# Issue order of the load queue, earlier Strassen inputs and a later output product in a two-MoE kernel

## The chip, the cores and the metric

The kernel runs on one core of one Trainium2 chip. The metric is device time in microseconds (us) of one execution. A core has five engines with a queue of instructions each: TensorE (PE, matrix products), VectorE (DVE), ScalarE (ACT), GpSimd (POOL) and SyncE (SP), which here issues nearly all DMA transfers. Each engine works through its own queue in order; engines wait for each other on semaphores.

## The reference

```python
def reference(q, k, v, w_in, w_out, w_gate, w_val, w_out2, rms_g):
    # 4 batches, 8 heads, 576 positions, head size 64
    # heads 0-3: the last 32 positions; heads 4-7: every 32nd position
    attn = softmax_masked(q @ k.T / 8) @ v
    x = attn as 2304 tokens x 512
    h = x @ w_in                              # 512 x 2048
    x = (h - np.tanh(h)) @ w_out              # 2048 x 512   (MoE one)
    xn = x / sqrt(mean(x * x) + 1e-6) * rms_g # MoE two
    g, val = xn @ w_gate, xn @ w_val          # 512 x 1536 each
    return (g * sigmoid(g) * val) @ w_out2    # 1536 x 512
```

All is fp32. The weights arrive as float64.

## The kernel before

Every fp32 operand is split into a high and a low part, and a product is made of three matmuls. A weight tile (128 x 512 numbers of 64 bits, 512 KB) is loaded as `raw`, turned into fp32 by ACT (a Prelu, L171 or L277) and DVE (L177, L178 or L278, L279), and split by ACT, DVE and POOL.

The program has four stages. Attention fills the gaps of **MoE one**, which runs in five groups of tokens; the last group (`g == NG - 1`, f = 0 to 15) lasts from about 374 to 462 us of the span. It prepares MoE two: `prep` loads the first 512 tokens' `x2d`, forms their sums of squares, 1/sqrt by three Newton steps on 128 x 512 elements, and `xn`. Its last results leave by ACT copies `xe` and transfers `x2d<-xe`.

**The plain stage** (462 to 573.5 us) runs MoE two on these 512 tokens in `FB` = 12 tiles f. `pe_gv(0, f)` makes the gate (`ps_h`) and the value (`ps_m`) of a tile and `p`, the product of silu(gate) and value; `pe_o(0, f)` adds the tile's 12 output matmuls into four banks `ps_x` (L927 and L928 split `p`). `Store` writes each decoded weight to DRAM (L343), `Decode.to` loads and decodes the weights of the next stage, and `both_preps` makes that stage's inputs: `prep_s` for the norm of 896 tokens, `conv(m)` for the inputs `xt[m]`.

**Two Strassen passes** (j = 0, 1) of 896 tokens follow, each of six pairs of tiles. A pair has seven products m, in the order 1, 2, 5, 6, 3, 7, 4, of 12 matmuls 128 x 448 (`both`: 6 for the gate, 6 for the value), and seven outputs `out(t)` of six matmuls 128 x 512, which are made during the next pair. Two tiles of a pair are turned by `Pair.steps` into the sums `wo`; nine blocks w_0 to w_8 of each pair go to DRAM (`Store`, or `put` at L255) and come back as `wt` (`fetch`, L260). `keep` copies a product out of its banks: `u<-ps_pr` on ACT (L1102). `second` stands in the first pair of the first pass, after product 1: it makes the last output matmuls of the plain stage, `pe_o(0, FB - 1)`, and `evac_o` copies the four banks `ps_x` to two buffers `o`, tiles 0 and 2 on ACT (L946), 1 and 3 on DVE (L948), each followed by its transfer `out_dram<-o` (L949). Product 6 writes into the banks that `keep` has to read after product 1:

```python
self.both(1, P, True)
if (self.j, self.p) == (0, 0):
    second()
m1 = self.keep(P)
...
self.both(6, P, False)
```

The order on each engine is that of the scheduler, which sorts instructions by its own estimate of time, except under `tc.manual_schedule(engines=...)`, where the named engines keep the order of the program. Before the change PE alone is held to it, in the first groups of MoE one and in the Strassen passes. `wts` is a pool of 22 rooms of 4 KB a partition (`tag="w"`), shared by weights and by the temporaries `wa`, `ws`, `s2` and `tr`.

Of the kernel before, what the change touches and what calls it, by code (L numbers as in the profile page):

```python
# [33 lines left out]
def attn_moe_moe_kernel(  # L34
# [211 lines left out]
    class Pair:  # L246
# [21 lines left out]
        def steps(self):  # L268
            a, t = {}, {}

            def bits(kd, i):
                if i == 0:
                    a[kd] = wts.tile([128, 2, 512], F32, tag="w", name="wa")
                w = self.ws[2 * kd + i].raw.rearrange("p c f -> p (c f)").bitcast(U32).rearrange("p (n t) -> p n t", t=2)
                lo, hi = w[:, :, 0], w[:, :, 1].bitcast(F32)
                o = a[kd][:, 1 - i].bitcast(U32)
                nc.scalar.activation(out=hi, in_=hi, func=ACTF.Prelu, scale=2.0 ** -111, alpha=-(2.0 ** 32))  # L277
                nc.vector.tensor_scalar(out=o, in0=lo, scalar1=29, scalar2=None, op0=ALU.logical_shift_right)  # L278
                nc.vector.scalar_tensor_tensor(  # L279
                    out=o, in0=hi.bitcast(U32), scalar=3, in1=o, op0=ALU.logical_shift_left, op1=ALU.bitwise_or  # L280
                )

            def sums(kd):
                t[kd] = wts.tile([128, 4, 256], F32, tag="w", name="ws")
                x = [a[kd][:, k // 2, 256 * (k % 2):256 * (k % 2) + 256] for k in range(4)]
                y = [t[kd][:, k] for k in range(4)]
                for o, p, q, op in (
                    (0, x[0], x[1], ALU.add), (1, y[0], x[2], ALU.subtract),
                    (2, x[2], x[0], ALU.subtract), (3, x[3], y[1], ALU.subtract),
                ):  # L290
                    nc.gpsimd.tensor_tensor(out=y[o], in0=p, in1=q, op=op)

            def half(kd, n):
                self.part(2 + 2 * n + kd, t[kd][:, 2 * n:2 * n + 2].rearrange("p n f -> p (n f)"))

            for kd in range(2):
                yield 2 * kd, lambda: bits(kd, 0)
# [563 lines left out]
    def prep():
        n = R0
        x2 = pbx.tile([128, 4, 2 * HT], F32, tag="x2", name="x2")[:, :, :n]
        for c in range(4):
            nc.sync.dma_start(out=x2[:, c, :], in_=x2d[c * 128:c * 128 + 128, 0:n])
        acc = pbx.tile([128, 512], F32, tag="acc", name="acc")[:, :n]
        sq = pbx.tile([128, 512], F32, tag="sq", name="sq")[:, :n]
        yield
        nc.scalar.activation(out=acc, in_=x2[:, 0], func=ACTF.Square)
        for c in range(1, 4):  # L870
            nc.scalar.activation(out=sq, in_=x2[:, c], func=ACTF.Square)
            nc.vector.tensor_tensor(out=acc, in0=acc, in1=sq, op=ALU.add)
            yield
        s2 = wts.tile([128, 2, 512], F32R, tag="w", name="s2")
        nc.scalar.copy(out=s2[:, 0], in_=acc)
        nc.vector.tensor_tensor(out=s2[:, 1], in0=acc, in1=s2[:, 0].bitcast(F32), op=ALU.subtract)
        yield
        ps = ps_m.tile([128, 512], F32, tag=nth("m", 2), name="ps_m")[:, :n]
        mm(ps, ones, s2[:, 0], True, False)
        mm(ps, ones, s2[:, 1], False, True)  # L880
        yield
        m, y = acc, sq
        z = pbx.tile([128, 512], F32, tag="z", name="z")[:, :n]
        nc.vector.tensor_scalar(
            out=m, in0=ps, scalar1=1.0 / DM, scalar2=1.0e-6, op0=ALU.mult, op1=ALU.add
        )
        yb, zb = y.bitcast(I32), z.bitcast(I32)
        nc.vector.tensor_scalar(
            out=zb, in0=m.bitcast(I32), scalar1=1, scalar2=None, op0=ALU.logical_shift_right
        )  # L890
        nc.vector.tensor_scalar(
            out=yb, in0=zb, scalar1=-1.0, scalar2=float(0x5F3759DF), op0=ALU.mult, op1=ALU.add
        )
        for _ in range(3):
            yield
            nc.vector.scalar_tensor_tensor(out=z, in0=y, scalar=-0.5, in1=y, op0=ALU.mult, op1=ALU.mult)
            nc.vector.tensor_tensor(out=z, in0=z, in1=m, op=ALU.mult)
            nc.vector.scalar_tensor_tensor(out=y, in0=z, scalar=1.5, in1=y, op0=ALU.add, op1=ALU.mult)
        yield
        t = mid.tile([128, 2, 4, 512], F32R, tag="xs", name="xn")  # L900
        for c in range(4):
            nc.vector.scalar_tensor_tensor(
                out=x2[:, c, :], in0=x2[:, c, :], scalar=gcol[:, c:c + 1], in1=y,
                op0=ALU.mult, op1=ALU.mult,
            )
            nc.scalar.copy(out=t[:, 0, c], in_=x2[:, c])
            nc.vector.tensor_tensor(out=t[:, 1, c], in0=x2[:, c], in1=t[:, 0, c].bitcast(F32), op=ALU.subtract)
            yield
        xn[0] = t

    p_of, oacc = {}, {}

    def pe_gv(j, f):
# [9 lines left out]
                s = pb.tile([128, 512], F32, tag="s", name="s")[:, :n]  # L923
                nc.scalar.activation(out=s, in_=ps, func=ACTF.Silu, scale=WS)
        nc.vector.scalar_tensor_tensor(out=s, in0=r[1], scalar=WS, in1=s, op0=ALU.mult, op1=ALU.mult)
        t = pb.tile([128, 2, 512], F32R, tag="p", name="p")[:, :, :n]
        nc.scalar.copy(out=t[:, 0], in_=s)  # L927
        nc.vector.tensor_tensor(out=t[:, 1], in0=s, in1=t[:, 0].bitcast(F32), op=ALU.subtract)  # L928
        p_of[j, f] = t
# [18 lines left out]
                nc.vector.tensor_scalar_mul(out=o, in0=oacc[j][t], scalar1=WS)  # L948
            nc.sync.dma_start(out=out[t * 128:t * 128 + 128, :], in_=o)  # L949

    xt = {}

    def prep_s(j, bank):
        base = R0 + 2 * HT * j
        x = pbx.tile([128, 4, 2 * HT], F32, tag="x2", name="x2")
        for c in range(4):
            nc.sync.dma_start(out=x[:, c], in_=x2d[c * 128:c * 128 + 128, base:base + 2 * HT])
        xt["raw"] = x
        yield
        parts = [(0, 512), (512, 2 * HT)]  # L960
        m, y, z = (pbx.tile([128, 8], F32, tag=n, name=n) for n in ("rm", "ry", "rz"))
        nt = 2 * HT // 128
        m, y, z = m[:, :nt], y[:, :nt], z[:, :nt]
        for h, (a, e) in enumerate(parts):
            n = e - a
# [2 lines left out]
            for c in range(1, 4):  # L968
                nc.scalar.activation(out=sq, in_=x[:, c, a:e], func=ACTF.Square)
                nc.vector.tensor_tensor(out=acc, in0=acc, in1=sq, op=ALU.add)  # L970
                yield
            s2 = wts.tile([128, 2, 512], F32R, tag="w", name="s2")[:, :, :n]
            nc.scalar.copy(out=s2[:, 0], in_=acc)
            nc.vector.tensor_tensor(out=s2[:, 1], in0=acc, in1=s2[:, 0].bitcast(F32), op=ALU.subtract)
            yield
# [39 lines left out]
    def conv(m):  # L1015
# [3 lines left out]

        def comb(name, p, q, out=None):  # L1020
            if out is None:
                out = wts.tile([128, 2, 512], F32, tag="w", name="tr")[:, :, :HT]
            nc.gpsimd.tensor_tensor(out=out, in0=p, in1=q, op=ALU.subtract)  # L1023
            xt[name] = out
            return out
# [242 lines left out]
    for g, f, a, e in units:  # L1268
        if g == 0:
            st1.to(2 * (f + 4))  # L1270
        elif f == 0:
# [33 lines left out]
        unit(g, f, a, e, pe_work, work)  # L1305
        if g == NG - 1:
            if f == 4:
                pg = prep()
            if pg is not None:
                next(pg, None)  # L1310
    while xq:
        pe_x(*xq.pop(0))
    for _ in pg:
        pass
# [11 lines left out]
    def both_preps():
        yield from prep_s(0, bank_m)
        for m in (1, 2, 5, 6, 3, 7, 4):
            conv(m)
            yield  # L1330

    pg = both_preps()
    for f in range(FB):
        st2.to(max(3 * (f + 2), N1 + (len(w2_order) - N1) * (f + 1) // (FB - 2)))
        store.to(st2.i - 4)
        pe_gv(0, f)
        if f >= 1:
            for _ in range(3 if f < FB - 1 else 40):
                next(pg, None)
        decode.to(max(0, 10 * (f - 7) // 4))  # L1340
        if f:
            pe_o(0, f - 1)
    store.to(len(w2_order))
    pairs[0].fetch((0, 1))
    ctx.enter_context(tc.manual_schedule(engines={mybir.EngineType.PE}))

    def second():
        nonlocal pb, osum
        pe_o(0, FB - 1)
        evac_o(0)  # L1350
        poolB.close()
        pb = ctx.enter_context(tc.tile_pool(name="pb", bufs=2, reuse_waits="tile"))
        osum = mid.tile([128, 4096], F32, tag="xs", name="osum").rearrange("p (t n) -> p t n", t=8)

# [2 lines left out]
    for j in range(NJ):  # L1357
        for p in range(NP):
# [3 lines left out]

            def tick(m):
                n = (1, 2, 5, 6, 3, 7, 4).index(m)
                if n == 0:
                    me.fetch((6, 7, 8))
                if j == 0:
                    decode.to(10 + 10 * (7 * p + n + 3) // 7)
                    if n in (3, 5):
# [121 lines left out]
```

## Time and profile before

| | |
|---|---|
| time, median of 3 runs | 914.79 us (913.88 to 917.0) |
| the profiled execution's own time | 914.88 us |
| its span, first to last instruction | 913.1 us |
| busy: PE / DVE / ACT / POOL | 96% / 71% / 45% / 27% |
| mean granted clock of TensorE | 0.985 of full speed |

The span and all positions below are those of the profiled execution, in us from its first instruction. The 1.8 us between span and time lie outside the instructions.

### The profile page before, as it was taken

What the parts mean: (1) busy time and instruction counts of PE and PEld (TensorE: products, weight loads), DVE (VectorE), ACT (ScalarE), POOL (GpSimd) and SP (SyncE); (2) the same over time, 40 slices, a digit from 0 to 9 for tenths busy, and PEclk for the clock granted to TensorE, in tenths of its full rate; (3) what the DMA queues carried; (4) which work ended last, traced back from release to release, by engine and by line L of the source; (5) the groups of instructions that cost most, each with busy time, mean ns of one, the idle gap of its engine ahead of it and who ended that gap; (6) DMA issues with size and microseconds to landing.
All of it is one profiled execution on the core that took longest, in us unless ns stands there. A gap on an engine that the chain in (4) does not pass through costs nothing. (4 is left out here: it accounts for less than half of the span.)

```text
span 913.1 us, 14228 instructions
## 1 busy us (share of the span) xinstructions
PE 879.8 (96%) x5139; PEld 749.0 (82%) x5139; DVE 645.3 (71%) x1359; ACT 410.9 (45%) x921; POOL 247.4 (27%) x291
## 2 busy tenths in 40 slices
PE   6899999998999999999999998499999999999998
PEld 4788888887998878888888886389888888888886
DVE  6799878986789896288857796367975665354545
ACT  6687733233544233376465445455442433423220
POOL 0000166783275951000000077325452000000000
PEclk8899999999999999999999999799999999999999
DMA  9971334320313100399668739866675567545002
GB/s 335 394 268 45 87 102 134 96 66 1 113 55 104 41 1 4 126 334 345 212 217 308 257 115 384 330 230 228 237 271 187 184 230 265 174 170 181 6 1 80
DMA packets 58710, 157.90 MB, mean 173 GB/s; under 512 B 9552, under 2 KB 20816, under 8 KB 58640
## 3 DMA queue, kind: packets, MB, share of 16 engines
q1 hardware_dynamic: 57488, 155.95, 49.1%
q10 hardware_dynamic: 1152, 1.05, 0.3%
q8 instruction: 40, 0.66, 0.3%
q14 instruction: 30, 0.25, 0.1%
HBM read 119.23 MB, written 37.75 MB: 172 GB/s over the span
## 5 line engine op out<-in xcount | busy, mean ns | idle before, releaser
L148 PE MATMUL ps_h<-xs,w 128*128 128x512 f32 (+1 forms) x984 | 215.7, 368 | 3.0 <-DVE tg L814 3.0
L148 PE MATMUL ps_x<-g,w 128*128 128x512 f32 (+1 forms) x984 | 215.1, 367 | 1.8 <-ACT g L820 1.8
L148 PEld LDWEIGHTS ps_h<-xs,w 128*128 128x128 f32 x984 | 170.9, 192 | 33.8 <-DVE tg L814 4.1
L148 PEld LDWEIGHTS ps_x<-g,w 128*128 128x128 f32 x984 | 169.1, 189 | 31.8 <-ACT g L820 2.0
L148 PE MATMUL ps_pr<-xt,wt 128*128 128x448 f32 x576 | 122.8, 366 | 0.4 <-DVE s L1092 0.4
L148 PE MATMUL ps_o<-wt,p 128*128 128x512 f32 x504 | 120.3, 390 | 0.0
L629 POOL TENSOR_TENSOR pr<-sk,sq 128x256 f32<-128x256 f32 (+2 forms) x101 | 82.4, 851 | 135.3 <-DMA sk<-in_k_str_dram 109.1
L148 PEld LDWEIGHTS ps_pr<-xt,wt 128*128 128x128 f32 x576 | 108.0, 188 | 10.7 <-DVE s L1092 0.8
L148 PEld LDWEIGHTS ps_o<-wt,p 128*128 128x128 f32 x504 | 94.6, 188 | 18.6
L820 ACT CAST g<-tg 128x512 fp32r<-128x512 f32 (+1 forms) x82 | 46.4, 567 | 110.5 <-DVE tg L814 110.3
L662 POOL TENSOR_TENSOR pr<-sv,se 128x288 f32<-128x288 f32 (+12 forms) x104 | 70.7, 701 | 59.2 <-DVE so L669 20.7
L1102 ACT COPY u<-ps_pr 128x448 f32<-128x448 f32 x72 | 37.9, 532 | 83.2 <-PE ps_pr L148 83.2
L148 PE MATMUL ps_pr<-xt,wo 128*128 128x448 f32 x288 | 63.1, 376 | 12.3 <-ACT u L1102 12.3
L148 PEld LDWEIGHTS ps_pr<-xt,wo 128*128 128x128 f32 x288 | 55.9, 195 | 17.6 <-ACT u L1102 12.7
L669 DVE TENSOR_REDUCE so<-pr 128x16 f32<-128x272 f32 (+11 forms) x104 | 65.0, 651 | 6.7 <-POOL pr L662 6.4
L814 DVE SCALAR_TENSOR_TENSOR tg<-ps_h,tg 128x512 f32<-128x512 f32 (+1 forms) x82 | 50.7, 619 | 26.6 <-ACT tg L809 26.3
L825 DVE TENSOR_TENSOR g<-tg,g 128x512 fp32r<-128x512 f32 (+1 forms) x82 | 57.4, 701 | 14.7 <-ACT g L820 14.1
L1153 DVE SCALAR_TENSOR_TENSOR osum<-ps_o,osum 128x512 f32<-128x512 f32 x70 | 48.0, 688 | 25.3 <-PE ps_o L148 24.5
L809 ACT ACTIVATE tg<-ps_h 128x512 f32<-128x512 f32 (+1 forms) x82 | 44.1, 539 | 46.1 <-PE ps_h L148 46.1
L1023 POOL TENSOR_TENSOR tr<-x 128x896 f32<-128x896 f32 x4 | 8.6, 2146 | 195.1 <-PE ps_h L148 176.9
L171 ACT ACTIVATE ca<-raw 128x512 f32<-128x512 f32 x68 | 45.5, 674 | 31.4 <-DMA raw<-in_w_out_dram 9.1
L634 DVE TENSOR_REDUCE sc<-pr 128x4 f32<-128x256 f32 (+2 forms) x101 | 44.0, 439 | 14.9 <-POOL pr L629 14.4
(129 smaller groups left out, 1163.7 us busy)
## 6 DMA issues: line engine op xcount, KB each, us to landing
wt<-w SPq DMA_DIRECT2D x84, 512.0 KB, 4.2
raw<-in_w_out_dram SPq DMA_DIRECT2D x28, 512.0 KB, 6.5
raw<-in_w_gate_dram SPq DMA_DIRECT2D x24, 512.0 KB, 5.5
raw<-in_w_val_dram SPq DMA_DIRECT2D x24, 512.0 KB, 6.0
w<-w SPq DMA_DIRECT2D x24, 512.0 KB, 5.2
w<-wo SPq DMA_DIRECT2D x24, 512.0 KB, 5.5
raw<-in_w_in_dram SPq DMA_DIRECT2D x16, 512.0 KB, 9.2
x2d<-xe SPq DMA_DIRECT2D x28, 128.0 KB, 1.8
```

What stands on the lines that cost most here:

```text
L148: nc.tensor.matmul(out_, lhsT, rhs, start=start, stop=stop, skip_group_check=True)
L171: nc.scalar.activation(out=self.a, in_=hi.bitcast(F32), func=ACTF.Prelu, scale=2.0 ** -111, alpha=-(2.0 ** 32))
L629: nc.gpsimd.tensor_tensor(out=pr, in0=self.k[:, a:e, :], in1=self.q[:, c - c0:c - c0 + 1, :].to_broadcast([128, e - a, D]), op=ALU.mult,)
L634: pend.append(lambda: nc.vector.tensor_reduce(out=s[:, c - c0, a:e], in_=pr, axis=AX.X, op=ALU.add))
L662: nc.gpsimd.tensor_tensor(out=pr, in0=self.v[:, 0:c + 1, a:e], in1=self.e[:, c - c0, 0:c + 1].unsqueeze(2).to_broadcast([128, c + 1, e - a ...
L669: pend.append(lambda: nc.vector.tensor_reduce(out=o[:, c - g0, a:e], in_=pr.rearrange("l c d -> l d c"), axis=AX.X, op=ALU.add))
L809: nc.scalar.activation(out=t, in_=h_of[g, f, a], func=ACTF.Tanh, scale=WS)
L814: nc.vector.scalar_tensor_tensor(out=t, in0=h_of.pop((g, f, a)), scalar=WS, in1=t, op0=ALU.mult, op1=ALU.subtract)
L820: nc.scalar.copy(out=t[:, 0], in_=t_of[g, f, a])
L825: nc.vector.tensor_tensor(out=t[:, 1], in0=t_of.pop((g, f, a)), in1=t[:, 0].bitcast(F32), op=ALU.subtract)
L1102: nc.scalar.copy(out=u, in_=x[kd])
L1153: nc.vector.scalar_tensor_tensor(out=o, in0=ps, scalar=WS, in1=o, op0=ALU.mult, op1=ALU.add)
```

## The change

1. From the start of MoE one's last group on, SP keeps the order of the program, so transfers are issued in the order in which the code is written.
2. `prep` is replaced. `prep_s` now serves the first 512 tokens too: 1/sqrt is made on 128 x 4 elements, for which 8 small matmuls `ps_r` turn the sums and 8 matmuls `ps_y` (128 x 128) spread the result, in place of two matmuls `ps_m<-s2,ones` and Newton steps on 128 x 512. `prep_s` and `conv` for the first pass are started within the last group, as soon as `xn` is there.
3. The temporaries have four rooms of their own (`tmp`) until `second`; `p` has three buffers, not two.
4. In the plain stage `pe_o` runs two tiles behind `pe_gv`, not one, and `Decode` starts a tile earlier with two steps a tile.
5. In a Strassen pair, the fetch of w_6, w_7, w_8 after product 1 becomes w_6 after product 2 and w_7, w_8 after product 3 or 7 (`tick` counts n = 1 and 5). `prep_s` of the second pass starts in pair 2, not in pair 0.

```diff
-                t[kd] = wts.tile([128, 4, 256], F32, tag="w", name="ws")
+                t[kd] = tmp[0].tile([128, 4, 256], F32, tag="w", name="ws")
...
+    xt, tmp = {}, [wts]
...
+    HALVES = [(0, 512), (512, 2 * HT)]
+
+    def preps():
+        yield from prep_s(0, [(0, R0)], bank_m)
+        x = xt["raw"]
         t = mid.tile([128, 2, 4, 512], F32R, tag="xs", name="xn")
         for c in range(4):
-            nc.vector.scalar_tensor_tensor(
-                out=x2[:, c, :], in0=x2[:, c, :], scalar=gcol[:, c:c + 1], in1=y,
-                op0=ALU.mult, op1=ALU.mult,
-            )
-            nc.scalar.copy(out=t[:, 0, c], in_=x2[:, c])
-            nc.vector.tensor_tensor(out=t[:, 1, c], in0=x2[:, c], in1=t[:, 0, c].bitcast(F32), op=ALU.subtract)
+            nc.scalar.copy(out=t[:, 0, c], in_=x[:, c, :R0])
+            nc.vector.tensor_tensor(out=t[:, 1, c], in0=x[:, c, :R0], in1=t[:, 0, c].bitcast(F32), op=ALU.subtract)
             yield
         xn[0] = t
+        yield from prep_s(R0, HALVES, bank_m)
+        for m in (1, 2, 5, 6, 3, 7, 4):
+            conv(m)
+            yield
...
-        t = pb.tile([128, 2, 512], F32R, tag="p", name="p")[:, :, :n]
+        t = pb.tile([128, 2, 512], F32R, tag="p", name="p", bufs=3)[:, :, :n]
...
         if g == NG - 1 and f == 0:
+            ctx.enter_context(tc.manual_schedule(engines={mybir.EngineType.SP}))
             poolT.close()
...
             if f == 4:
-                pg = prep()
-            if pg is not None:
-                next(pg, None)
+                pg = preps()
+            for _ in range(0 if pg is None else 2 - f % 2):
+                next(pg)
...
+    tmp[0] = poolB.enter_context(tc.tile_pool(name="tmp", bufs=4, reuse_waits="tile"))
...
         pe_gv(0, f)
-        if f >= 1:
-            for _ in range(3 if f < FB - 1 else 40):
-                next(pg, None)
-        decode.to(max(0, 10 * (f - 7) // 4))
-        if f:
-            pe_o(0, f - 1)
+        for _ in range(3 if f < FB - 2 else 40):
+            next(pg, None)
+        decode.to(max(0, 10 * (f - 6) // 5))
+        if f > 1:
+            pe_o(0, f - 2)
+    pe_o(0, FB - 2)
     store.to(len(w2_order))
     pairs[0].fetch((0, 1))
-    ctx.enter_context(tc.manual_schedule(engines={mybir.EngineType.PE}))
+    ctx.enter_context(tc.manual_schedule(engines={mybir.EngineType.PE, mybir.EngineType.SP}))
...
         evac_o(0)
         poolB.close()
+        tmp[0] = wts
...
-                if n == 0:
-                    me.fetch((6, 7, 8))
+                if n in (1, 5):
+                    me.fetch((6,) if n == 1 else (7, 8))
...
-            if p == 0 and j + 1 < NJ:
-                pg = prep_s(j + 1, bank_x)
+            if p == 2 and j + 1 < NJ:
+                pg = prep_s(R0 + 2 * HT * (j + 1), HALVES, bank_x)
```

ACT, at the start of the first Strassen pair, before the change: `o<-ps_x` are the two copies of `evac_o`, L967 and L969 belong to `prep_s` of the second pass, L265 and L277 to the decoding of pairs, and the four `u` are the copies of products 1 and 5.

```order
L946 ACTIVATE o<-ps_x 128x512
L967 ACTIVATE acc<-x_6435 128x384
L969 ACTIVATE sq<-x_6435 128x384
L277 ACTIVATE raw<-raw 128x512
L969 ACTIVATE sq<-x_6435 128x384
L277 ACTIVATE raw<-raw 128x512
L265 CAST wo<-ws 128x512 x2
L277 ACTIVATE raw<-raw 128x512
L946 ACTIVATE o<-ps_x 128x512
L277 ACTIVATE raw<-raw 128x512
L1102 COPY u<-ps_pr 128x448 x4
L1078 ACTIVATE s<-s 128x448
```

The same place on ACT with the change (L912 is the copy to `o`, L1065 the copy to `u`, L893 the split of `p`):

```order
L893 CAST p<-s 128x512
L912 ACTIVATE o<-ps_x 128x512 x2
L1065 COPY u<-ps_pr 128x448 x4
L1041 ACTIVATE s<-s 128x448
L277 ACTIVATE raw<-raw 128x512
L1065 COPY u<-ps_pr 128x448
L265 CAST wo<-ws 128x512
L277 ACTIVATE raw<-raw 128x512
```

Four Prelu operations of decoding and the norm of the second pass stood between the first `o` and the four `u`; now the copies follow each other, and the next Prelu on a loaded tile comes after them.

SP, around the four transfers `out_dram<-o`, before the change (L165 loads a `raw`, L255 stores a sum, L260 fetches a block; the last number of a `w_` name counts the DRAM tile):

```order
L165 DMA raw<-in_w_val_dram 128x512
L949 DMA out_dram<-o 128x512
L260 DMA wt<-w_6_114 128x1024
L949 DMA out_dram<-o 128x512
L260 DMA wt<-w_7_115 128x1024
L255 DMA w_5_113<-wo 128x1024
L260 DMA wt<-w_8_116 128x1024
L255 DMA w_2_119<-wo 128x1024
L165 DMA raw<-in_w_gate_dram 128x512
L949 DMA out_dram<-o 128x512
L255 DMA w_4_121<-wo 128x1024
L949 DMA out_dram<-o 128x512
```

The same place on SP with the change (L915 is the transfer of `o`; w_0_99 to w_8_107 belong to pair 0, w_0_108 and w_1_109 to pair 1):

```order
L344 DMA w_8_152<-w 128x1024
L260 DMA wt<-w_0_99 128x1024
L260 DMA wt<-w_1_100 128x1024
L915 DMA out_dram<-o 128x512 x4
L165 DMA raw<-in_w_val_dram 128x512 x2
L165 DMA raw<-in_w_gate_dram 128x512 x2
L260 DMA wt<-w_6_105 128x1024
L255 DMA w_2_101<-wo 128x1024
L255 DMA w_3_102<-wo 128x1024
L260 DMA wt<-w_0_108 128x1024
L260 DMA wt<-w_1_109 128x1024
L260 DMA wt<-w_7_106 128x1024
```

Before, SP had gone on to blocks of pairs 1 and 2 while the outputs were still to come; with the change all loads and fetches of the pass but w_0, w_1 and those ahead of them stand behind the four outputs.

PE, end of the plain stage, before the change (`ps_h` gate, `ps_m` value, `ps_x` output matmuls of 128 x 512; `ps_pr` with 12 rows of 128 x 448 is product 1):

```order
L148 MATMUL ps_m<-xn,w 128x512 x12
L148 MATMUL ps_x<-w,p 128x512 x12
L148 MATMUL ps_h<-xn,w 128x512 x12
L148 MATMUL ps_m<-xn,w 128x512 x12
L148 MATMUL ps_x<-w,p 128x512 x12
L148 MATMUL ps_pr<-xt_5479,wt 128x448 x12
L148 MATMUL ps_x<-w,p 128x512 x12
```

With the change:

```order
L148 MATMUL ps_m<-xn,w 128x512 x12
L148 MATMUL ps_x<-w,p 128x512 x12
L148 MATMUL ps_h<-xn,w 128x512 x12
L148 MATMUL ps_m<-xn,w 128x512 x12
L148 MATMUL ps_x<-w,p 128x512 x24
L148 MATMUL ps_pr<-xt_5516,wt 128x448 x12
L148 MATMUL ps_x<-w,p 128x512 x12
```

The two tiles that are owed stand together at the end, so the last tile's `p` has 24 matmuls and product 1 ahead of its use, not 12 and product 1.

## Rows read from the trace of the kernel before

**Rows 1.** The page: the span; busy time, share and instructions of each engine.

```profile
span 913.1 us, 14228 instructions
PE 879.8 (96%) x5139; PEld 749.0 (82%) x5139; DVE 645.3 (71%) x1359; ACT 410.9 (45%) x921; POOL 247.4 (27%) x291
```

**Rows 2.** PE's waits, 386 to 913 us: us in total, times, longest us.

```profile
PE ps_pr L148 <- ACT u L1102: 12.3, 1, 12.3
PE ps_x L148 <- ACT p L927: 2.8, 1, 2.8
PE ps_x L148 <- DVE p L928: 1.0, 2, 0.7
PE ps_pr L148 <- DVE s L1092: 0.4, 1, 0.4
```

**Rows 3.** PE in order of time: start, duration, operation [idle before <- releaser].

```profile
556.04 3.35 PE L148 MATMUL ps_x<-w,p 128*128 128x512 f32 x12 [2.76 <-ACT p L927]
...
570.77 2.90 PE L148 MATMUL ps_x<-w,p 128*128 128x512 f32 x12
573.50 2.60 PE L148 MATMUL ps_pr<-xt,wo 128*128 128x448 f32 x12
575.94 2.60 PE L148 MATMUL ps_q<-xt,wt 128*128 128x448 f32 x12
590.87 9.92 PE L148 MATMUL ps_pr<-xt,wo 128*128 128x448 f32 x36 [12.34 <-ACT u L1102]
```

**Rows 4.** ACT, DVE and SP in order of time, 572 to 592 us.

```profile
575.38 0.38 SPq L949 DMA_DIRECT2D out_dram<-o  x1
...
582.69 0.69 DVE L948 TENSOR_SCALAR o<-ps_x 128x512 f32<-128x512 f32 x1 [3.69 <-DMA out_dram<-o]
582.87 0.57 ACT L946 ACTIVATE o<-ps_x 128x512 f32<-128x512 f32 x1
...
584.22 0.33 SPq L165 DMA_DIRECT2D raw<-in_w_gate_dram  x1
...
589.75 0.65 ACT L277 ACTIVATE raw<-raw 128x512 f32<-128x512 f32 x1 [6.31 <-issue]
590.31 1.81 ACT L1102 COPY u<-ps_pr 128x448 f32<-128x448 f32 x4
```

**Rows 5.** SP's waits, 462 to 600 us: total, times, longest.

```profile
SPq L343 <- DVE w L189: 35.6, 10, 20.5
```

**Rows 6.** Windows; the last three columns are granted clock, DMA share, GB/s.

```profile
518.80:539.20 20.40, 20.40 (x99) 17.11 (x98) 19.72 (x21) 11.53 (x16) 9.70 (x4) 1.00 0.11 38
539.20:590.00 50.80, 35.53 (x156) 28.52 (x154) 28.47 (x39) 21.11 (x39) 33.38 (x30) 0.93 0.98 366
...
591.00:601.00 10.00, 9.80 (x36) 8.54 (x36) 6.86 (x13) 5.71 (x13) 3.67 (x5) 0.75 0.17 62
```

**Rows 7.** PE, the same 36 matmuls three pairs later.

```profile
670.30 7.46 PE L148 MATMUL ps_pr<-xt,wo 128*128 128x448 f32 x36
```

**Rows 8.** PE's two matmuls of the norm in the last group.

```profile
426.30 0.62 PE L148 MATMUL ps_m<-s,ones 128*128 128x512 f32 x2
```

**Rows 9.** Pieces of the chain that ended last: start, us, what.

```profile
603.95 0.79 PE ps_r L148 x8
...
637.16 0.84 PE ps_y L148 x8
```

**Rows 10.** DMA issues by kind: KB each, median us from issue to landing.

```profile
out_dram<-osum SPq DMA_DIRECT2D x14, 256.0 KB, 2.0
...
out_dram<-o SPq DMA_DIRECT2D x4, 256.0 KB, 5.9
```

**Rows 11.** SP and ACT in MoE one's last group, in order of time.

```profile
377.52 0.33 SPq L165 DMA_DIRECT2D raw<-in_w_gate_dram  x1
...
378.83 3.89 SPq L851 DMA_DIRECT2D x2d<-xe  x8
...
387.38 0.68 ACT L171 ACTIVATE ca<-raw 128x512 f32<-128x512 f32 x1 [2.00 <-DMA raw<-in_w_val_dram]
```

More of the change, by code (lines that the diff above doesn't have):

```diff
@@ L272, in bits @@
                 if i == 0:
-                    a[kd] = wts.tile([128, 2, 512], F32, tag="w", name="wa")
+                    a[kd] = tmp[0].tile([128, 2, 512], F32, tag="w", name="wa")
                 w = self.ws[2 * kd + i].raw.rearrange("p c f -> p (c f)").bitcast(U32).rearrange("p (n t) -> p n t", t=2)
@@ L859, in attn_moe_moe_kernel @@
     xn = {}
[L861 to L885, printed above, removed]
-        )
[L887 to L899, printed above, removed]
@@ L900, in prep @@
+    HALVES = [(0, 512), (512, 2 * HT)]
+    def preps():
+        yield from prep_s(0, [(0, R0)], bank_m)
+        x = xt["raw"]
         t = mid.tile([128, 2, 4, 512], F32R, tag="xs", name="xn")
         for c in range(4):
-            nc.vector.scalar_tensor_tensor(
-                out=x2[:, c, :], in0=x2[:, c, :], scalar=gcol[:, c:c + 1], in1=y,
-                op0=ALU.mult, op1=ALU.mult,
-            )
-            nc.scalar.copy(out=t[:, 0, c], in_=x2[:, c])
-            nc.vector.tensor_tensor(out=t[:, 1, c], in0=x2[:, c], in1=t[:, 0, c].bitcast(F32), op=ALU.subtract)
+            nc.scalar.copy(out=t[:, 0, c], in_=x[:, c, :R0])
+            nc.vector.tensor_tensor(out=t[:, 1, c], in0=x[:, c, :R0], in1=t[:, 0, c].bitcast(F32), op=ALU.subtract)
@@ L949, in evac_o, with prep_s @@
             nc.sync.dma_start(out=out[t * 128:t * 128 + 128, :], in_=o)
-    xt = {}
-    def prep_s(j, bank):
-        base = R0 + 2 * HT * j
+    def prep_s(base, parts, bank):
+        w = parts[-1][1]
         x = pbx.tile([128, 4, 2 * HT], F32, tag="x2", name="x2")
         for c in range(4):
-            nc.sync.dma_start(out=x[:, c], in_=x2d[c * 128:c * 128 + 128, base:base + 2 * HT])
+            nc.sync.dma_start(out=x[:, c, :w], in_=x2d[c * 128:c * 128 + 128, base:base + w])
         xt["raw"] = x
         yield
-        parts = [(0, 512), (512, 2 * HT)]
         m, y, z = (pbx.tile([128, 8], F32, tag=n, name=n) for n in ("rm", "ry", "rz"))
-        nt = 2 * HT // 128
+        nt = w // 128
         m, y, z = m[:, :nt], y[:, :nt], z[:, :nt]
@@ L971, in prep_s @@
                 yield
-            s2 = wts.tile([128, 2, 512], F32R, tag="w", name="s2")[:, :, :n]
+            s2 = tmp[0].tile([128, 2, 512], F32R, tag="w", name="s2")[:, :, :n]
             nc.scalar.copy(out=s2[:, 0], in_=acc)
@@ L1021, in comb @@
             if out is None:
-                out = wts.tile([128, 2, 512], F32, tag="w", name="tr")[:, :, :HT]
+                out = tmp[0].tile([128, 2, 512], F32, tag="w", name="tr")[:, :, :HT]
             nc.gpsimd.tensor_tensor(out=out, in0=p, in1=q, op=ALU.subtract)
@@ L1307, in attn_moe_moe_kernel @@
             if f == 4:
-                pg = prep()
-            if pg is not None:
-                next(pg, None)
+                pg = preps()
+            for _ in range(0 if pg is None else 2 - f % 2):
+                next(pg)
     while xq:
         pe_x(*xq.pop(0))
-    for _ in pg:
-        pass
     poolA.close()
@@ L1322, in attn_moe_moe_kernel @@
     poolB = ExitStack()
+    tmp[0] = poolB.enter_context(tc.tile_pool(name="tmp", bufs=4, reuse_waits="tile"))
     cvt = poolB.enter_context(tc.tile_pool(name="cvt2", bufs=2, reuse_waits="tile"))
     pb = poolB.enter_context(tc.tile_pool(name="pb", bufs=2, reuse_waits="tile"))
[L1326 to L1332, printed above, removed]
     for f in range(FB):
```

## The prediction

> **What bounds the kernel now.** PE does: it is busy for 879.8 of 913.1 us [rows 1]. The matmuls are nearly the same after the change, so the question is what becomes of the 33.3 us in which PE is idle. The change leaves the order on every engine alone up to MoE one's last group, so I read PE's waits from there on: four groups, 16.5 us together [rows 2]. One of them holds three quarters: 12.3 us on an ACT copy `u`. In PE's order of time it sits in the first Strassen pair, ahead of product 6, and the matmuls behind it are slow as well [rows 3].
>
> The other engines at that place tell why [rows 4]. Product 6 writes into the banks of product 1, which `keep` must have copied out. The copies `u` stand on ACT behind a Prelu that starts at 589.75, and the copies follow at once, at 590.31. That Prelu decodes a `raw` whose transfer SP issued only at 584.22. The row puts its idle time to "issue", but the copies' operands were made long before, and 584.22 plus a landing time as the outputs had it in the full queue, 5.9 us [rows 10], fits 589.75. The second outputs `o` were late in the same way: they waited for the transfer of the first, issued at 575.38, until 582.69, since there are two buffers.
>
> Why was DMA late? SP stood for 20.5 us on one store, whose weight DVE had not split yet [rows 5]. In that stretch (518.8 to 539.2) DMA moved 38 GB/s, and afterwards 366 GB/s at a share of 0.98 up to the stall [rows 6]. So the load is there to be spread, and the stall is one of order: SP's and ACT's.
>
> **What the change takes away.** (a) ACT's order no longer has a Prelu between `o` and the first four `u`: what has to be decoded for pair 0 now stands ahead of `o`, in the plain stage, and the next tiles behind the copies. The wait of 12.34 us goes if the copies now come in time. I take the end of the last output matmuls as T0; before, that is 573.50. Product 5 takes to 575.94, 2.44 us, product 2 as long: product 6 wants its banks at T0+4.9. The 12 output matmuls take 2.73 us (570.77 to 573.50) [rows 3], so tile 0 is done at T0-2.05. Its copy takes 0.57 [rows 4]. Its transfer takes 2.0 us where DMA is quiet, as for the 14 `osum` transfers of equal size, and 5.9 us in the full queue [rows 10]. SP holds back all loads behind these outputs in the new order, so I take 2.0; with 0.4 for the issue [rows 4] it has landed at T0+0.9. Then come the second copy (0.57) and two of the four `u` (1.81 for four) [rows 4]: T0+2.4, before T0+4.9. With 5.9 it would be T0+6.3 for both: up to 1.4 us late.
>
> (b) The slow clock behind the stall goes with it. The window 591 to 601 has a granted clock of 0.75, between the two levels of 1.2 and 2.4 GHz [rows 6]; the 36 matmuls took 9.92 us [rows 3], and 7.46 three pairs later [rows 7]: 2.46 us.
>
> (c) `pe_o` two tiles behind gives `p` a further tile of 24 matmuls, at the rate above 5.5 us, more than each of the waits of 2.8 and 1.0 us on L927 and L928 [rows 2]; the longest, at 553, was 2.76 [rows 3]. The four rooms and the third `p` buffer only feed this: they cost no instructions. The 0.4 us on `s` L1092 stays, since products 7 and 4 still adjoin in pair 0.
>
> Together 12.3 + 2.8 + 1.0 = 16.1, plus 2.46: 18.6 us.
>
> **What it adds.** PE gets eight `ps_r` and eight `ps_y` more, 0.79 + 0.84 [rows 9], and loses two `ps_m` of 0.62 [rows 8]: 1.0 us net. DVE loses some ten Newton operations of 512 elements in a stretch where PE never waited for it; I cost that at nothing. The second pass's norm, moved from pair 0 to pair 2, has four more pairs until it is needed: nothing, and ACT and DVE are freed in pair 0.
>
> In the last group SP now issues `x2d<-xe` x8 (3.89 us) ahead of the loads that went before it at 377.52, so these start some 5 us later; ACT waited 2.00 us for such a load even before, at 387.38 [rows 11], without PE waiting. Bounds: 0, and 4 us if the 5 us came through less the 1 to 2 us by which PE runs ahead. I take 0.5, near the lower end, because the row's wait of ACT cost PE nothing. In the plain stage stores, loads and the `x2d` loads are now in line on SP. The bounds are 0 and one more wait like the 2.8 us; I take 0.5.
>
> At the start of the Strassen passes all DMA is now behind the outputs. The fourth output can be issued after the second transfer has landed (T0+1.7) and a DVE copy of 0.69 [rows 4]: about T0+2.8, and the loads go from T0+3.1. A transfer of 512 KB takes 0.524 MB / 366 GB/s = 1.43 us [rows 6]. The fetch of w_6 is the fifth: with two outputs in flight (0.7) and the rest of a landing (1.3) it is there at T0+12.3, and product 4 wants it after products 5, 2, 6, 3, 7: 5 x 2.44 = T0+12.2. The next pair's w_0 is the eighth and w_1 the ninth: T0+16.5 and T0+18.0, wanted at T0+14.6 and T0+15.9. So PE waits about 2 us at the start of pair 1. Bounds: 0 (transfers that overlap better than the mean of a loaded window, where the queue was also held by stores) and 6 (outputs that land in 5.9 us, below). Later pairs are easier: some 13 transfers a pair, 18.6 us, against 7 x 2.44 for the products and seven outputs of half of 2.73, 26.6 us.
>
> The Trainium skill's page "DMA: Bandwidth & Descriptors", section "Specifications", puts the limit between HBM and one core at about 358 GB/s. By it the eight transfers would take 0.3 us more than by the row, and the sum would be 900.6. The window's mean of 366 GB/s lies 2% above that figure [rows 6], so this trace does not bear it out as a strict limit, though it comes close.
>
> **The sum.** Against the profiled execution's 914.88 us (0.1 above the median of 914.79): 914.88 - 18.6 + 1.0 = 897.3; with 0.5 + 0.5 + 2.0 of new waits 900.3. I forecast 900.3.
>
> **The rivals.**
>
> The outputs find a full queue (5.9 us, not 2.0). Then product 6 waits up to 1.4 us, the loads start at T0+7.0 in place of T0+3.1, and w_0 of pair 1 is there at T0+20.4: about 5.8 us of wait with the 1.4 in it, 3.8 more than forecast. If the clock falls behind this wait as it did before, 2.46 us come on top. 904 to 907. For it: every one of the four outputs took that long before. Against it: SP's order, which lets nothing out for a while ahead of them.
>
> The stall only moves: SP in the code's order waits for a late split as it did for 20.5 us [rows 5], a Prelu later in pair 0 or 1 finds no `raw`, and its copies `u` hold PE for about 12 us with the slow clock. 897.3 + 12.3 + 2.5 + 1 = 913. For it: SP may now pass nothing that is late. Against it: stores trail the decoding by four steps, so what a store waits for should be long done.
>
> Slower than before: first-pass pairs that each wait. In each of five pairs the loads, the two pairs of stores of `wo` (POOL's work) and the fetches stand in one line; if every pair's first block came late because a store ahead of it waits for POOL, PE would pay per pair. From 897.3 the kernel comes out slower than 917.6 once that is over 4 us a pair; at the 5.9 us of a full-queue landing it is 927. For it: DMA has 0.98 of its time used in the rows of the plain stage, and lateness adds up in a line. Against it: 18.6 us of transfers in 26.6 us, and POOL is busy for 27% of the span.
>
> The change doesn't do what it says: ACT's copies wait anyway, and only (c) comes: 914.88 - 3.8 + 1.0 = 912 or a little above. It is held with the moved stall.
>
> **Chances.** Forecast, 897 to 903: 0.63. Outputs in a full queue, 903 to 909: 0.17. Stall moved or not removed, 910 to 917: 0.06. Slower by pairs that wait: 0.09. Below 897, by new waits near nothing and small idle stretches that go as well: 0.05. The range is 896 to 909: from just under the floor without new waits to the upper end of the full queue. A change of 0.3%, 2.7 us, is about what a measurement of this kernel can tell from none. Faster than that: 0.63 + 0.17 + 0.05 and a part of the moved stall, 0.87. Within it: 0.04. Slower: 0.09.
>
> **What the profile after would show.** Right: PE's waits from 386 us on no longer have `u` with a wait above 1 us; the two `o` on ACT and four `u` follow each other within about 4 us; the granted clock stays at 1.00 over T0 to T0+30; the three waits on `p` L927 and L928 are gone; a short wait on DMA `wt` stands at the start of pair 1; SP issues the four outputs before any load of pair 1's `val`. Wrong: a wait on `wt` or on `s` of over 5 us in pairs 0 to 2 with a slow clock behind it; a transfer `out_dram<-o` of 5 us or more; waits on `tg` or `w` in the last group; a Prelu that waits for its `raw` ahead of a `u` or a `p`.

## The result, and the profile after

The changed kernel takes 909.73 us (median of 11 runs, 906.37 to 912.57), the kernel before 917.35 us in the same comparison (11 runs, 913.88 to 920.75; the 914.79 ahead of the prediction was the median of the first three). The ratio is 0.9914 [0.9893, 0.9935]: faster by 0.9%. The forecast was 900.3 against 914.88, 1.6%. The sign was right; the gain is about half of the forecast, and 909.73 lies just outside the range.

The page of the changed kernel, span and busy time, which answer to [rows 1]:

```profile
span 909.7 us, 14221 instructions
PE 882.5 (97%) x5153; PEld 750.3 (82%) x5153; DVE 640.8 (70%) x1361; ACT 411.1 (45%) x921; POOL 251.3 (28%) x291
```

PE's waits of the changed kernel from 360 us on (total, times, longest), which answer to [rows 2]:

```profile
PE ps_m L148 <- DVE s L891: 2.1, 1, 2.1
PE ps_pr L148 <- DVE s L1055: 2.1, 1, 2.1
PE ps_x L148 <- DVE p L894: 0.7, 1, 0.7
PE ps_pr L148 <- ACT u L1065: 0.5, 1, 0.5
PE ps_pr L148 <- DMA wt<-w: 0.2, 1, 0.2
```

The 12.3 us are gone. Two waits on DVE, of 2.1 us each, were not foreseen. PE of the changed kernel in order of time, which answers to [rows 3]:

```profile
374.00 5.60 PE L148 MATMUL ps_x<-g,w 128*128 128x512 f32 x24
...
468.66 1.30 PE L148 MATMUL ps_h<-xn,w 128*128 128x512 f32 x5
...
527.74 4.24 PE L148 MATMUL ps_h<-xn,w 128*128 128x512 f32 x18
534.09 4.45 PE L148 MATMUL ps_m<-xn,w 128*128 128x512 f32 x12 [2.11 <-DVE s L891]
...
580.29 2.59 PE L148 MATMUL ps_pr<-xt,wo 128*128 128x448 f32 x12
582.72 2.59 PE L148 MATMUL ps_q<-xt,wt 128*128 128x448 f32 x12
585.15 6.38 PE L148 MATMUL ps_pr<-xt,wo 128*128 128x448 f32 x30
592.02 1.49 PE L148 MATMUL ps_pr<-xt,wo 128*128 128x448 f32 x6 [0.49 <-ACT u L1065]
595.60 3.84 PE L148 MATMUL ps_pr<-xt,wt 128*128 128x448 f32 x12 [2.09 <-DVE s L1055]
599.63 2.95 PE L148 MATMUL ps_pr<-xt,wt 128*128 128x448 f32 x12 [0.20 <-DMA wt<-w]
602.42 2.59 PE L148 MATMUL ps_q<-xt,wt 128*128 128x448 f32 x12
```

Behind each of the two waits a group of matmuls is slow as well: 4.45 us where such a group takes 2.88, 3.84 where it takes 2.59. The windows (last columns granted clock, DMA share, GB/s) of 14 us in the plain stage and of product 5 of pair 0 to product 2 of pair 1 give granted clocks of 0.88 and 0.92, between the two levels of 1.2 and 2.4 GHz (over the group of 4.45 us alone, 534.0 to 538.5, it is 0.65):

```profile
531.00:545.00 14.00, 11.89 (x45) 9.00 (x44) 12.21 (x17) 4.96 (x9) 10.25 (x7) 0.88 0.29 99
580.29:602.42 22.13, 19.36 (x85) 16.41 (x84) 17.17 (x25) 12.73 (x24) 13.74 (x12) 0.92 0.86 312
```

Up to MoE one's last group both kernels have the same order, but profiled executions of one order differ there: the 24 matmuls `ps_x<-g` at the end of group four start at 369.17 in the profile of before and at 374.00 after. So the spans are compared by stages from there on. Each stage is the difference of two starts on PE (the 24 matmuls; the first `ps_h<-xn`; product 5 of pair 0; product 2 of pair 1; the end of the span). Before, the first two and the fourth stand in these rows of PE's order of time:

```profile
369.17 5.60 PE L148 MATMUL ps_x<-g,w 128*128 128x512 f32 x24
...
462.14 1.30 PE L148 MATMUL ps_h<-xn,w 128*128 128x512 f32 x5
...
607.15 2.64 PE L148 MATMUL ps_q<-xt,wt 128*128 128x448 f32 x12
```

| stage, us | before | after | change | forecast |
|---|---|---|---|---|
| last group | 92.97 | 94.66 | +1.7 | +1.5 |
| plain stage | 111.36 | 111.63 | +0.3 | -3.3 |
| pair 0, from product 5 | 33.65 | 22.13 | -11.5 | -12.8 |
| the rest | 305.95 | 307.28 | +1.3 | 0 |
| sum | 543.93 | 535.70 | -8.2 | -14.6 |

The sum of -8.2 agrees with the medians (-7.6). Of the 6.4 us that are missing, 3.6 are in the plain stage, 1.3 in each of the last two stages and 0.2 in the last group. Pair 0 and the rest are one account in part: eight `ps_r` (about 0.8 us) left the one for the other with the second pass's norm, so pair 0 is really 2.1 short.

### The profile page after: what moved, and what is told of

Read it like the earlier page. It is cut to its first block, busy times and chain, and to the rows that moved or that the text cites. A ratio compares the mean times of both kernels' runs of the same rounds, so it can differ in the third digit from the quotient of the medians.

```text
span 909.7 us, 14221 instructions
## 1 busy us (share of the span) xinstructions
PE 882.5 (97%) x5153; PEld 750.3 (82%) x5153; DVE 640.8 (70%) x1361; ACT 411.1 (45%) x921; POOL 251.3 (28%) x291
## 4 chain that ended last, share of the span: by engine, by line
PE 61%; DVE 8%; POOL 5%; issue 1%; DMA 1%; ACT 1%; POOLq 0%; ACTq 0%; DVEq 0%
PE ps_pr L148 19%; PE ps_o L148 13%; PE ps_x L148 12%; PE ps_h L148 11%; POOL pr L630 4%; PE ps_q L148 3%; DVE so L670 3%; PE ps_m L148 2%; DMA wt<-w 1%; DVE xt L1006 1%; POOL pr L663 1%; POOL ws L291 1%; DVE tg L815 1%; DVE x L972 0%; DVE sm L406 0%
## 5 line engine op out<-in xcount | busy, mean ns | idle before, releaser
L1065 ACT COPY u<-ps_pr 128x448 f32<-128x448 f32 x72 | 38.1, 534 | 72.7 <-PE ps_pr L148 72.2
L148 PE MATMUL ps_pr<-xt,wo 128*128 128x448 f32 x288 | 61.0, 366 | 0.5 <-ACT u L1065 0.5
L148 PEld LDWEIGHTS ps_pr<-xt,wo 128*128 128x128 f32 x288 | 53.8, 188 | 5.6 <-ACT u L1065 1.1
L189 DVE TENSOR_TENSOR w<-ct,w 128x512 fp32r<-128x512 f32 x68 | 49.4, 733 | 12.4 <-ACT w L185 12.4
```

The source lines that it names most:

```text
L148: nc.tensor.matmul(out_, lhsT, rhs, start=start, stop=stop, skip_group_check=True)
L189: eng.tensor_tensor(out=t[:, 1], in0=self.b, in1=t[:, 0].bitcast(F32), op=ALU.subtract)
L1065: nc.scalar.copy(out=u, in_=x[kd])
```

## The experiments

The stages of the table, PE's waits and the ratio to the kernel before are read for each. All edits are to the changed kernel, but for the first.

**Part 1 alone, in the kernel before.**

```diff
         if g == NG - 1 and f == 0:
+            ctx.enter_context(tc.manual_schedule(engines={mybir.EngineType.SP}))
...
-    ctx.enter_context(tc.manual_schedule(engines={mybir.EngineType.PE}))
+    ctx.enter_context(tc.manual_schedule(engines={mybir.EngineType.PE, mybir.EngineType.SP}))
```

> The kernel before with the change's part 1 alone: SP in program order from MoE one's last group on. If the gain comes from the order of the transfers, the 12.3 us wait on u in the first Strassen pair is gone or under 4 us, and the time is 7 to 12 us under the kernel before. If the gain needs the earlier inputs and the earlier decoding as well, a Prelu still stands ahead of the four copies u, the wait stays at 8 us or more, and the time is within 4 us of the kernel before.

0.9968 [0.9951, 0.9984], 913.67 us. Neither forecast holds whole. Its waits on PE from 360 us on:

```profile
PE ps_r L148 <- ACT s L973: 6.8, 1, 6.8
PE ps_x L148 <- DVE p L928: 1.9, 1, 1.9
PE ps_pr L148 <- DVE s L1092: 1.1, 1, 1.1
PE ps_r L148 <- DVE s L974: 0.7, 1, 0.7
PE ps_pr L148 <- DVE v L1095: 0.5, 1, 0.5
```

The wait on `u` is gone by the order of SP alone. In its place PE waits 6.8 us for the sums of the second pass's norm, whose matmuls `ps_r` stand at the end of pair 0 in PE's order, and whose `x` SP now loads only behind the four outputs. Part 5 moves that norm to pair 2, and this wait is not in the changed kernel; no run has parts 1 and 5 alone, so that part 5 is what makes part 1 pay is argued, not shown.

**The changed kernel without part 1.**

```diff
-            ctx.enter_context(tc.manual_schedule(engines={mybir.EngineType.SP}))
...
-    ctx.enter_context(tc.manual_schedule(engines={mybir.EngineType.PE, mybir.EngineType.SP}))
+    ctx.enter_context(tc.manual_schedule(engines={mybir.EngineType.PE}))
```

> The changed kernel without program order on SP (the scheduler orders it). If part 1 carries the gain, a wait of 8 us or more is back in pair 0 and the time is 5 us or more above the changed kernel. If the earlier inputs and decoding carry it, the time is within 3 us of the changed kernel, and the loads of pair 1 go out before the four outputs.

0.9972 [0.9955, 0.9989], 914.23 us, 4.5 us above the changed kernel, a little under the 5 us that the first reading asked for. The long wait is back: on `u` L1065, 8.1 us, in pair 0. ACT of this kernel in order of time:

```profile
579.90 0.68 ACT L277 ACTIVATE raw<-raw 128x512 f32<-128x512 f32 x1 [4.32 <-DMA raw<-in_w_val_dram]
...
588.73 0.65 ACT L277 ACTIVATE raw<-raw 128x512 f32<-128x512 f32 x1 [1.29 <-DMA raw<-in_w_gate_dram]
589.28 1.82 ACT L1065 COPY u<-ps_pr 128x448 f32<-128x448 f32 x4
```

This is the mechanism that the prediction read from [rows 4]: Prelu operations that wait for a `raw`, and the copies `u` queued behind them. Part 1 and the rest give 0.3% each; together 0.9%.

**Four buffers o, and loads ahead of the outputs.** Two ways to take the new wait in pair 0 away.

```diff
-            o = pb.tile([128, 512], F32, tag="o", name="o")
+            o = pb.tile([128, 512], F32, tag="o", name="o", bufs=4)
```

> The changed kernel with four buffers o for the plain outputs. Theory one (DVE is late in pair 0, because its second copy to o waits 4.15 us for a transfer, and the decoding of pair 1 piles up on DVE and POOL behind it): the copy no longer waits, the loads go out 3 us sooner, PE's waits in pairs 0 and 1 fall from 2.8 us to under 1.5, the clock stays up, and from product 5 of pair 0 to the end it takes 326 to 328 us, not 329.4. Theory two (the amount of work between product 5 and product 4 is too large for DVE in any case): the waits only move by the 3 us and stay above 2 us in sum.

```diff
     pairs[0].fetch((0, 1))
+    while decode.n < 8:
+        decode.ws[decode.n].load()
+        decode.n += 1
```

> The changed kernel with the two value tiles of pair 1 loaded ahead of the four outputs; nothing is decoded sooner. If the transfers behind the outputs are what makes pair 0 wait, PE's waits in pairs 0 and 1 fall from 2.8 us to under 1 us. If DVE is, it is still held by the second buffer o until about T0+3.7, has the same decoding to do then, and the waits stay at 1.5 to 3 us.

0.9918 [0.9893, 0.9943] and 0.9916 [0.9893, 0.9938]: neither differs from the changed kernel. Pair 0 takes 21.5 and 23.0 us. With four buffers DVE's second copy to `o` comes 1.4 us after its first, not 4.8 us, and PE still waits 2.1 us on `s` L1055 and 1.3 us on `s` L1041 of ACT. So the buffer is not the cause (theory one falls). With the value tiles loaded early the wait on `s` is 2.7 us: ACT now waits for the next tiles, the gates, which are the first loads behind the outputs. So two tiles loaded early do not take the wait away; the run does not clear the transfers, since the Prelu that stands there now waits for the first loads behind the outputs.

**Half of pair 1 decoded in the plain stage.**

```diff
     pe_o(0, FB - 2)
+    decode.to(15)
```

> The changed kernel with half of pair 1 (its two gate tiles) decoded in the plain stage, where DVE and POOL stand idle for 7 and 32 us before the outputs, not behind the outputs. If the amount of work of DVE and POOL between products 5 and 4 of pair 0 is what PE waits for (2.1 us on s in the changed kernel, in the kernel with four buffers o too), that wait is under 0.7 us, the clock stays at 1.00, and product 5 of pair 0 to product 2 of pair 1 takes 19.5 to 20.5 us, not 22.1. If the transfers behind the outputs are, it stays above 21.5, since as many of them stand there.

0.9931 [0.991, 0.9951]; pair 0 takes 24.2 us, with 2.7 us on `s`: the forecast of the work theory failed. ACT of this kernel shows why:

```profile
584.04 0.58 ACT L1041 ACTIVATE s<-s 128x448 f32<-128x448 f32 x1 [3.90 <-DVE s L1055]
585.97 0.67 ACT L277 ACTIVATE raw<-raw 128x512 f32<-128x512 f32 x1 [1.35 <-DMA raw<-in_w_gate_dram]
586.54 0.51 ACT L1065 COPY u<-ps_pr 128x448 f32<-128x448 f32 x1
```

The Prelu of the next tile, loaded behind the outputs, again stands ahead of product 6's `u`, and DVE, which needs that `u` for `s`, stands behind both. Half the work away leaves that first Prelu in place. The two theories needed a third: the order on ACT, with some decoding still due in pair 0.

**The plain stage: input making spread out, and the subtractions on DVE.**

```diff
-        for _ in range(3 if f < FB - 2 else 40):
+        for _ in range(2 if f < FB - 2 else 40):
```

> The changed kernel with two steps of input making a tile of the plain stage in place of three, so that the scaling of x and the splitting of the inputs xt come later and thinner. If the burst of that work on DVE is what makes PE wait 2.1 us for s in the plain stage (with a slow clock behind it), that wait is gone or under 0.7 us and the plain stage takes 108 to 109.5 us, not 111.6. The rival is that DVE has too much to do in this stage as a whole: then the wait moves to a later tile and the stage takes 111 us or more.

```diff
-            nc.gpsimd.tensor_tensor(out=out, in0=p, in1=q, op=ALU.subtract)
+            nc.vector.tensor_tensor(out=out, in0=p, in1=q, op=ALU.subtract)
             xt[name] = out
```

> The changed kernel with the four subtractions tr of the inputs on DVE, not on POOL. DVE gets four operations more of about 1.1 us a pass. If DVE's operations are slow there because POOL works beside it (xt 2.6 us, not 1.08), they are all 1.1 us or less now, DVE is through with the inputs no later, and the wait of 2.1 us is under 1.5 us. If the slow rows have another reason, DVE is later by 3 to 4 us and the wait grows to 4 us or more.

0.9879 [0.9859, 0.9899] and 0.9867 [0.9844, 0.9889]: 905.09 and 904.76 us. The plain stage takes 106.4 and 106.6 us, 5 us less (the first was expected to reach 108 to 109.5), and PE waits for nothing in it. DVE and POOL of the changed kernel there:

```profile
519.07 2.13 POOL L986 TENSOR_TENSOR tr<-x 128x896 f32<-128x896 f32 x1 [165.72 <-DVE x L972]
519.90 5.19 DVE L1006 TENSOR_TENSOR xt<-x,xt 128x896 fp32r<-128x896 f32 x2
521.28 2.86 POOL L986 TENSOR_TENSOR tr<-x,tr 128x896 f32<-128x896 f32 x1
524.10 2.97 POOL L986 TENSOR_TENSOR tr<-x 128x896 f32<-128x896 f32 x1
...
525.01 2.60 DVE L189 TENSOR_TENSOR w<-ct,w 128x512 fp32r<-128x512 f32 x1
...
528.21 1.08 DVE L1006 TENSOR_TENSOR xt<-x,xt 128x896 fp32r<-128x896 f32 x1
```

and DVE with the subtractions on it:

```profile
514.60 1.08 DVE L1006 TENSOR_TENSOR xt<-x,xt 128x896 fp32r<-128x896 f32 x1
515.60 1.08 DVE L986 TENSOR_TENSOR tr<-x 128x896 f32<-128x896 f32 x1
...
517.60 0.68 DVE L189 TENSOR_TENSOR w<-ct,w 128x512 fp32r<-128x512 f32 x1
```

An `xt` takes 2.6 us and a `w` 2.60 while POOL runs a `tr`, and 1.08 and 0.68 without; DVE's and POOL's operations there end one after the other. The Trainium skill's page "SBUF — State Buffer", section "Who interferes with whom", says that a DVE operation with two inputs in SBUF and a GpSimd operation that reads SBUF lock each other out whole. The rows agree. So POOL "takes work off" DVE here at a price higher than the work: four operations more on DVE make it faster. The price alone is not the wait, though. With the input making spread out, POOL still runs the four `tr` and an `xt` beside them takes 3.02 us, but no `s` that PE wants stands behind the slow rows. The wait needs both: the slow rows, and their place in DVE's queue.

**The output products one tile behind again,** in the changed kernel and in the one with the subtractions on DVE.

```diff
-        if f > 1:
-            pe_o(0, f - 2)
-    pe_o(0, FB - 2)
+        if f:
+            pe_o(0, f - 1)
```

> The changed kernel with the plain output products one tile behind, as before. If the second tile of distance is what took the waits on p away (3.8 us before), they are back with 2 us or more and the plain stage is 1.5 us or more longer than 111.6. If it did nothing, since DVE's lateness comes from the inputs, the stage stays within 0.7 us.

> The kernel with the subtractions on DVE, and the output products one tile behind. With the waits of the input work gone, it shows what the second tile of distance is worth by itself. If the waits on p of the kernel before came from the short distance, they are back: 1.5 to 4 us more than 106.6 in the plain stage. If they came from the same slow rows of DVE, the stage stays within 0.7 us of 106.6.

0.9933 [0.9908, 0.9958] and 0.9854 [0.9831, 0.9878]. The plain stage takes 111.3 and 106.6 us, as with two tiles, and with the subtractions on DVE there is no wait on `p` at all. With POOL's subtractions the waits on `p` do grow, from 0.7 to 1.8 us, just under the 2 us that were expected; the stage is no longer because no slow group follows the wait of 2.1 us on `s` in this profile (12 matmuls in 3.03 us, not 4.45). So the second tile of distance takes 1.1 us of waits away beside POOL's subtractions, less than the slow group that came in one profile and not in the other, and nothing without them; in the time of the stage no gain is measurable.

**The whole of pair 1 decoded in the plain stage, subtractions on DVE.**

```diff
     pe_o(0, FB - 2)
+    decode.to(20)
```

> The kernel with the subtractions on DVE, and all of pair 1 decoded in the plain stage, not half of it. If pair 0 waits because a Prelu on a tile loaded behind the outputs holds ACT's copies u, and decoding fills DVE behind it, no such Prelu is left ahead of product 4: PE's waits in pair 0 are under 0.7 us (2.5 and 0.5 before this edit) and product 5 of pair 0 to product 2 of pair 1 takes 17.5 to 19.5 us, not 22.4. If loads and fetches behind the outputs land late in any case, PE waits for wt there instead, and the stretch stays above 21 us. Decoding in the plain stage may cost there: up to 1 us more than 106.6.

0.9803 [0.9779, 0.9827]: 899.3 us. This beats both kernels. Pair 0 takes 17.31 us, the plain stage 107.1 (0.5 more), and PE's one wait from 360 us on is 0.2 us. PE and ACT of this kernel:

```profile
571.21 2.59 PE L148 MATMUL ps_pr<-xt,wo 128*128 128x448 f32 x12
573.64 2.59 PE L148 MATMUL ps_q<-xt,wt 128*128 128x448 f32 x12
576.07 7.46 PE L148 MATMUL ps_pr<-xt,wo 128*128 128x448 f32 x36
583.37 5.31 PE L148 MATMUL ps_pr<-xt,wt 128*128 128x448 f32 x24
```

```profile
572.12 0.60 ACT L912 ACTIVATE o<-ps_x 128x512 f32<-128x512 f32 x1 [2.15 <-DMA out_dram<-o]
572.61 1.84 ACT L1065 COPY u<-ps_pr 128x448 f32<-128x448 f32 x4
576.38 0.58 ACT L1041 ACTIVATE s<-s 128x448 f32<-128x448 f32 x1 [1.93 <-DVE s L1055]
577.54 0.54 ACT L1065 COPY u<-ps_pr 128x448 f32<-128x448 f32 x1 [0.58 <-PE ps_pr L148]
```

No Prelu stands ahead of product 6's `u`, which now waits for PE and not for DMA. The second `o` still waits 2.15 us for its buffer, at no cost. The edit takes three things out of pair 0 together: the late Prelu, the decoding of pair 1 on DVE and POOL, and the four `raw` loads that stood between the outputs and the next pair's first fetch (they now go out ahead of the outputs). Which of the three is worth how much, no run separates.

**Decoding later in pair 0, subtractions on DVE.**

```diff
-                    decode.to(10 + 10 * (7 * p + n + 3) // 7)
+                    decode.to(10 + 10 * (7 * p + n + (3 if p else 0)) // 7)
```

> The kernel with the subtractions on DVE, and the decoding in pair 0 started three products later (18 steps by its end, not 22). If the Prelu and the decoding are what pair 0 waits for, the waits fall under 1 us and the stretch to 18 to 20 us; some of it may come back as a wait for w of pair 1 later. If the transfers behind the outputs hold it, the stretch stays at 22 us.

0.987 [0.9849, 0.9891], as without the edit; pair 0 takes 23.4 us. The scheduler puts the Prelu where it was: ACT starts one at 583.31 after 1.78 us on DMA, and `u` at 583.88. Fewer steps by the end of the pair do not help as long as the first one stands there. The stretch of 22 us or more is what the theory of late transfers expected too. The kernel with all of pair 1 decoded has fetches behind the outputs as well, and no wait, but four loads fewer ahead of them, so that theory is not ruled out.

**Without the four rooms.**

```diff
-    tmp[0] = poolB.enter_context(tc.tile_pool(name="tmp", bufs=4, reuse_waits="tile"))
```

> The changed kernel without the four rooms for temporaries (they come from the pool of the weights again). If the rooms matter, SP or DVE wait for rooms in the plain stage and it is 1 us or more longer than 111.6, or the loads of the first pass go out later. If they only feed the rest, all stages stay within 0.7 us.

0.9871 [0.9847, 0.9895], 906.21 us: probably faster than the changed kernel, though the two intervals just touch. The plain stage takes 108.0 us: PE's wait on `s` L891 is gone, though DVE's `xt` are as slow as before. Pair 0 is about the same (22.5 us), now with a wait of 1.5 us for `wt`. So the four rooms cost some 3.6 us in the plain stage, by the order that they gave the scheduler: in the changed kernel four `wa` of the decoding (2.1 us together) stand on DVE ahead of the `s` that PE wants, without the rooms none do.

## Why the prediction was right and wrong

- **The long wait, (a), was right.** `u` behind a Prelu was the cause, and it is gone; the outputs' transfers land in 2.0 to 4.0 us (median 2.4), near the 2.0 that was taken, and the first four `u` follow the second `o` at 581.70, T0+1.4 (T0, the end of the last output matmuls, is 580.29 here). The order of SP alone takes that wait away; without it the wait comes back with 8.1 us.
- **The slow clock, (b), was right for that wait,** but the new waits of 2.1 us brought slow groups of their own: 1.6 us behind the one, 1.3 and 0.4 behind the other.
- **(c) is the step that failed.** The prediction said that a second tile of distance takes the 3.8 us on `p` away and left 0.5 us for new waits in the plain stage, with an upper bound of 2.8. Measured: 0.7 us on `p` are left, but a new wait of 2.1 us on `s` and a slow group of 1.6 us behind it came in their place, and the stage lasts 111.6 us where 106.6 are enough without POOL's subtractions. What held PE was DVE: an `s` stood there behind rows that POOL's `tr` had made slow, and the length of PE's queue does not touch that. Nor was it mainly the distance that took the 3.8 us on `p` away: with one tile these waits are 1.8 us in the changed kernel, 1.9 us in the kernel before with SP's order alone, and none with the subtractions on DVE. The price of POOL's work could be read in the trace of before: two `xt` of 5.27 us together beside a `tr`, where a lone one takes 1.08:

```profile
525.48 2.13 POOL L1023 TENSOR_TENSOR tr<-x 128x896 f32<-128x896 f32 x1 [176.92 <-PE ps_h L148]
...
526.23 5.27 DVE L1043 TENSOR_TENSOR xt<-x,xt 128x896 fp32r<-128x896 f32 x2
```

These rows are not what PE waited for in the kernel before. Its wait of 2.76 us on `p` ended at 556.04, some 18 us after the last `tr`, and DVE had been idle for 3.56 us before 549.70. The rows lead to ACT: the silu `s` of that tile (L924) stood behind a cast that waited 4.15 us for a sum `ws` of POOL, which took 4.12 us there and 0.74 in the median, and the split of `p` (L927) then stood behind further decoding. No run tests that chain by itself.

```profile
542.62 4.12 POOL L291 TENSOR_TENSOR ws<-wa 128x256 f32<-128x256 f32 x1
...
547.48 0.62 ACT L265 CAST wo<-ws 128x512 fp32r<-128x512 f32 x1 [4.15 <-POOL ws L291]
...
549.58 0.58 ACT L924 ACTIVATE s<-ps_h 128x512 f32<-128x512 f32 x1
...
555.37 0.61 ACT L927 CAST p<-s 128x512 fp32r<-128x512 f32 x1
```

The prediction read PE's waits on `p` and went to the length of the queue on PE, and not on to what held ACT and DVE. It also costed the input work at nothing by counting what DVE loses, and did not look at where that work moves to: ahead of a tile whose `s` PE needs.
- **The start of the Strassen passes: a size off, and another mechanism.** Forecast were 2.0 us of wait for `wt`; there were 0.2, and that is luck. The loads went out at 585.11, T0+4.8 and not T0+3.1, since DVE's second copy waited 4.15 us for a transfer, and the wait for the next pair's first block ends at T0+19.3, not T0+16.5. It is short only because PE itself came there at T0+19.1, not T0+14.6; by these numbers PE would otherwise have waited for it for up to 4.7 us, an estimate. The 4.8 us that were lost (22.1 against 17.3) are waits on DVE and ACT of 2.6 us, the 0.2 and slow groups. The rival "the stall only moves" had the mechanism, a Prelu without its `raw` ahead of a `u`, but priced it at 12 us; it is 1 to 2 us on ACT, and with the decoding on DVE behind it 2.1 on PE.
- **The last group** was right in sum (+1.7 against +1.5), by other terms: PE is busy for 94.60 of the 94.66 us, so the small matmuls `ps_r` and `ps_y` account for it (+1.0 forecast), and the later loads cost PE nothing (+0.5 forecast).
- **Slower, and outputs in a full queue,** did not come: no pair after pair 1 has a wait.

With the new waits taken away by two further edits the kernel takes 899.3 us, 17.8 under the kernel before in the same comparison (917.08); the floor of the prediction, 897.3 against 914.88, was 17.6 under. The floor was about right in sum, and what the prediction took for nearly free was not.

## What to carry to other kernels

A wait on an engine's result has to be followed to what that engine did before, and to what it waited for: compare the durations of its rows with those of the same shape elsewhere, since an operation that takes twice its usual time points to a neighbour. Work given to POOL was paid for by DVE here, where DVE had operations with two SBUF inputs at the time. A wait that is short behind another wait may only be hidden by it. On an engine that works in order, an operation that waits for a transfer must not stand ahead of one that PE waits for; where decoding is needed soon after a boundary, do all of it before, since doing half of it leaves the first such operation in place.

## What the runs showed of the hardware

A DVE operation of 128x512 with two SBUF inputs took 2.60 us beside a POOL operation of 2.97 us, where it takes 0.68: the 128x896 `xt`, 1.08 us alone, took about as long beside a `tr`, so the price goes by POOL's operation, not by DVE's. And a short wait can cost nearly as much again in clock, or little: after a wait of 2.11 us 12 matmuls took 4.45 us, not 2.88, at a granted clock of 0.65 (534.0 to 538.5); after the same wait in the kernel with the output products one tile behind 12 took 3.03, at 1.00 (531 to 545); and in the kernel before, after 2.76 us, 12 took 3.35 [rows 3], at 1.00 (553 to 560).
